# Attention products on two row halves of TensorE, padded leftovers and two pairs of heads at a time, in a linear-attention plus gated-FFN kernel

## The chip, the cores and the metric

One core of one Trainium2 chip runs the whole program. The metric is the device time of one execution in microseconds (us). Most executions agree within 0.3%. A profiled execution's span is about 1.8 us shorter than its measured time (838.4 against 840.17 for the kernel before).

## The reference

```python
kv  = einsum('bhsd,bhse->bhde', k, v)            # batch 8, heads 8, 576 tokens, 64 per head
out = einsum('bhsd,bhde->bhse', q, kv)
out = out / sqrt(mean(out*out, -1) + 1e-6) * g_norm
x   = out.transpose(0, 2, 1, 3).reshape(4608, 512)
h   = ((x @ w1) * (x @ w2)) @ w3                 # w1, w2: 512x1024, w3: 1024x1024
y   = h @ w_out                                  # 1024x512
```

All is fp32. 576 tokens are 512 plus a leftover of 64. The kernel folds `w3 @ w_out` into one 1024x512 matrix first (the "fold"), then runs eight tiles of 512 tokens and one of the eight leftovers through the FFN ("gates" and "projection", by a Winograd scheme of 2x2 blocks). The attention of the next batch is cut into pieces that stand between the gate matmuls. Batch 0's attention stands in the second half of the fold.

## The kernel before

Heads come in pairs (`r`, two heads `e`). k·v runs on two column halves of the array, one head each; the leftover has 64 rows:

```python
def kv(r):
    ...
    for j in range(J + 1):                     # 4 blocks of 128 tokens, then the leftover
        for e in range(2):
            nc.tensor.matmul(kv_ps[e * D:(e + 1) * D, :],
                lhsT=k_sb[:, e, cols] if j < J else kl_sb[:, 2 * r + e, :],   # kl_sb: 64 rows
                rhs=v_sb[:, e, cols] if j < J else vl_sb[:, 2 * r + e, :],
                start=(j == 0), stop=(j == J))
    ...                                        # copied twice, onto the diagonal of bd
```

q·kv uses that block-diagonal matrix, so that one full-array matmul serves two sets of 128 tokens, half of its products being with zeros:

```python
def product(r):
    o_ps = bank(ps_at, "at")
    for e in range(2):
        for i in range(2):
            n = 2 * e + i
            nc.tensor.matmul(o_ps[:, n * P:(n + 1) * P],
                lhsT=qT[r][:, e, i, :],        # 128 x 128
                rhs=bd[:, 2 * r + e, :],       # 128 x 128, block-diagonal
                start=True, stop=True)
    ...
    return norm(...)      # square, sum, root, reciprocal, scale: ScalarE and VectorE
```

The pieces of one batch, in the order in which they stand between gate matmuls (`begin`: k·v and the q transposes, `middle`: product and normalization, `turn`: transposes of the result), and batch 0's places among the eight steps of the fold:

```python
pieces = [[(begin, 0)], [(middle, 0), (begin, 1)], [(turn, 0), (middle, 1)], [(begin, 2), (turn, 1)],
          [(middle, 2), (begin, 3)], [(turn, 2), (middle, 3)], [(turn, 3)], []]
AT = {1: 0, 3: 1, 4: 2, 5: 3}      # fold step: pair of batch 0
ps_mm = ... bufs=5                 # PSUM banks for fold, gates and projection
ps_at = ... bufs=3                 # PSUM banks for attention and transposes
```

PSUM is the memory into which TensorE writes its results. The kernel takes it in eight tiles of 512 columns, here called banks.

## Time and profile before

| | before |
|---|---|
| median time | 839.25 us (3 runs; 839.14 with the rounds of the comparison) |
| span of the profile | 838.4 us |
| TensorE busy | 98% |
| VectorE, ScalarE busy | 46%, 32% |
| first gate matmul starts at | 91.16 us |
| from there to the end | 747.2 us |

The last two rows split the time at the first gate matmul. Ahead of it (the "start") weights are loaded and converted and the fold is done, with TensorE, VectorE and the DMA near their limits (from 16 to 49 us they are busy for 32.67, 31.02 and all of the 33 us). After it (the "main part") TensorE runs almost without a gap. Where a matmul stands in time is read from the timeline; the distance from one start to the next is its price, since matmuls are pipelined and a record's own length is a latency.

### The profile page before, as it was taken

What the parts mean: (1) busy time and instruction counts of PE and PEld (TensorE: products, weight loads), DVE (VectorE), ACT (ScalarE), POOL (GpSimd) and SP (SyncE); (2) the same over time, 40 slices, a digit from 0 to 9 for tenths busy, and PEclk for the clock granted to TensorE, in tenths of its full rate; (3) what the DMA queues carried; (4) which work ended last, traced back from release to release, by engine and by line L of the source; (5) the groups of instructions that cost most, each with busy time, mean ns of one, the idle gap of its engine ahead of it and who ended that gap; (6) DMA issues with size and microseconds to landing.
All of it is one profiled execution on the core that took longest, in us unless ns stands there. A gap on an engine that the chain in (4) does not pass through costs nothing.

```text
span 838.4 us, 11142 instructions
## 1 busy us (share of the span) xinstructions
PE 824.1 (98%) x4556; PEld 697.2 (83%) x4556; DVE 384.5 (46%) x770; ACT 268.5 (32%) x507; POOL 0.7 (0%) x6
## 2 busy tenths in 40 slices
PE   6999999999999999999999999999999999999997
PEld 4455788888888888888888888888888888888886
DVE  7978996415431544154315441453145404422430
ACT  5668443223312332133223321332133312211210
POOL 0000000000000000000000000000000000000000
PEclk9999999999999999999999999999999999999999
DMA  8999232022203220113022301230120010001002
GB/s 306 323 281 288 68 89 86 3 89 70 57 0 100 70 58 1 76 52 87 1 78 62 88 2 51 76 88 1 51 76 1 1 51 1 0 1 51 1 0 51
DMA packets 60002, 59.44 MB, mean 71 GB/s; under 512 B 15408, under 2 KB 56368, under 8 KB 59952
## 3 DMA queue, kind: packets, MB, share of 16 engines
q1 hardware_dynamic: 59792, 58.73, 22.6%
q8 instruction: 36, 0.59, 0.3%
q14 instruction: 14, 0.11, 0.1%
q10 hardware_dynamic: 160, 0.00, 0.0%
HBM read 49.28 MB, written 9.44 MB: 70 GB/s over the span
## 4 chain that ended last, share of the span: by engine, by line
PE 95%; DMA 2%; DVE 1%; ACT 1%; issue 0%; SPq 0%; ACTq 0%; DVEq 0%
PE mm L464 78%; PE mm L445 5%; PE at L337 3%; PE at L270 3%; PE at L292 2%; PE at L367 2%; DMA raw<-in_moe_w_out_dram 1%; DMA raw<-in_moe_w_dram 1%; PE at L354 1%; PE at L432 1%; DVE ab L151 0%; SPq L184 0%; PE at L376 0%; PE at L302 0%; DVE chunks L158 0%
## 5 line engine op out<-in xcount | busy, mean ns | idle before, releaser
L464 PE MATMUL mm<-xT,w_sb 128*128 128x256 f32 x768 | 176.2, 379 | 0.0
L464 PEld LDWEIGHTS mm<-xT,w_sb 128*128 128x128 f32 x768 | 145.9, 190 | 20.3 <-issue 0.5
L464 PE MATMUL mm<-xc,ws 128*128 128x256 f32 x576 | 130.2, 379 | 0.0
L464 PEld LDWEIGHTS mm<-xc,ws 128*128 128x128 f32 x576 | 109.4, 190 | 14.9
L477 ACT COPY u<-mm 128x512 f32<-128x512 f32 x90 | 52.8, 586 | 205.3 <-PE mm L464 190.6
L477 ACT COPY p<-mm 128x512 f32<-128x512 f32 x90 | 52.7, 586 | 138.9 <-PE mm L464 138.8
L464 PE MATMUL mm<-w3o_sb,ab 128*128 128x256 f32 x432 | 96.2, 379 | 0.0
L464 PEld LDWEIGHTS mm<-w3o_sb,ab 128*128 128x128 f32 x432 | 82.1, 190 | 11.2
L464 PE MATMUL mm<-xc,w_sb 128*128 128x256 f32 x288 | 68.1, 379 | 0.0
L445 PE MATMUL mm<-chunks,ab 128*128 128x512 f32 x128 | 62.6, 624 | 4.1 <-DVE chunks L161 4.1
L464 PE MATMUL mm<-raw 128*128 128x256 f32 x288 | 63.6, 379 | 0.0
L464 PEld LDWEIGHTS mm<-raw 128*128 128x128 f32 x288 | 54.7, 190 | 7.4
L464 PE MATMUL mm<-xT,ws 128*128 128x256 f32 x256 | 60.8, 380 | 0.0
L312 DVE TENSOR_REDUCE inv<-sq 128x8 f32<-128x512 f32 (+1 forms) x40 | 25.1, 629 | 73.3 <-ACT sq L310 73.3
L464 PEld LDWEIGHTS mm<-xc,w_sb 128*128 128x128 f32 x288 | 52.9, 190 | 6.2
L590 DVE TENSOR_TENSOR c<-mm,u 128x512 f32<-128x512 f32 x36 | 24.5, 681 | 61.2 <-PE mm L464 61.2
L464 PEld LDWEIGHTS mm<-xT,ws 128*128 128x128 f32 x256 | 46.5, 190 | 5.4
L619 DVE TENSOR_TENSOR raw<-mm,u 128x512 f32<-128x512 f32 x9 | 6.2, 692 | 97.3 <-PE mm L464 97.3
L591 DVE TENSOR_TENSOR ab<-c 128x256 f32<-128x256 f32 x108 | 45.6, 423 | 2.9
L445 PEld LDWEIGHTS mm<-chunks,ab 128*128 128x128 f32 x128 | 23.1, 200 | 27.3 <-issue 21.9
L590 DVE TENSOR_TENSOR c<-p,u 128x512 f32<-128x512 f32 x36 | 24.9, 691 | 34.3 <-ACT u L477 34.3
L284 DVE COPY kv_bd<-at 64x64 f32<-64x64 f32 x64 | 13.9, 217 | 55.8 <-PE at L270 55.2
(83 smaller groups left out, 856.6 us busy)
## 6 DMA issues: line engine op xcount, KB each, us to landing
raw<-in_moe_w_dram SPq DMA_DIRECT2D x31, 512.0 KB, 6.6
k_sb<-in_k_dram SPq DMA_DIRECT2D x32, 256.0 KB, 2.8
v_sb<-in_v_dram SPq DMA_DIRECT2D x32, 256.0 KB, 3.2
q_sb<-in_q_dram SPq DMA_DIRECT2D x32, 256.0 KB, 4.3
out_dram<-raw SPq DMA_DIRECT2D x16, 512.0 KB, 2.6
raw<-in_moe_w_out_dram SPq DMA_DIRECT2D x8, 512.0 KB, 8.3
kl_sb<-in_k_dram SPq DMA_DIRECT2D x8, 128.0 KB, 4.9
vl_sb<-in_v_dram SPq DMA_DIRECT2D x8, 128.0 KB, 4.6
```

What stands on the lines that cost most here:

```text
L270: nc.tensor.matmul(kv_ps[e * D:(e + 1) * D, :], lhsT=k_sb[:, e, cols] if j < J else kl_sb[:, 2 * r + e, :], rhs=v_sb[:, e, cols] if j < J ...
L284: nc.vector.tensor_copy(out=dst, in_=src)
L292: nc.tensor.transpose(qt_ps[:, e, i, :], q_sb[:, e, i * P:(i + 1) * P], ident)
L312: nc.vector.tensor_reduce(out=inv, in_=sq[:, cols].rearrange("p (h d) -> p h d", d=D), axis=AX.X, op=ALU.add,)
L337: nc.tensor.matmul(o_ps[:, n * P:(n + 1) * P], lhsT=qT[r][:, e, i, :], rhs=bd[:, 2 * r + e, :], start=True, stop=True,)
L354: nc.tensor.matmul(o_ps[l * L:(l + 1) * L, r * D:(r + 1) * D], lhsT=st["qT"][rows, r, l * L:(l + 1) * L], rhs=kv_bd[l][rows, 2 * r + e, rows],
L367: nc.tensor.transpose(t_ps[:, j, :], st[r][:, j], ident)
L445: nc.tensor.matmul(sums_ps[half][m], lhsT=w3T[half, c][:, m, :], rhs=chunks[:, c, 1, :], start=(c == 0), stop=(c == KF - 1),)
L464: nc.tensor.matmul(ps[:, u, :], lhsT=lhsT(a_name, u, c), rhs=rhs(b_name, c),  start=(u == 0 and c == 0 and to is None), stop=(c == chunks ...
L477: nc.scalar.copy(t, ps)
L590: nc.vector.tensor_add(c, one, two)
L591: nc.vector.tensor_mul(dst, c[:, 0, :], c[:, 1, :])
```

## The change

The author's intent: a contraction of 64 rows wastes half of a 128-row array, so run two of them at once on the two row halves, drop the zeros of the block-diagonal form, pad the leftover of k and v with zero rows so that its k·v needs no other array layout, and treat two pairs of heads at a time so that layouts change less often. The diff, cut to its core:

```diff
+    kv_left = [const.tile([P, H, D], FP32, name=f"{name}l_sb") for name in "kv"]
+    for t in kv_left:
+        nc.gpsimd.memset(t[L:P], 0.0)                 # rows 64 to 127 are zero
-    kv_bd = [const.tile([P, H, P], ...)]; memset
+    kv_sb = [const.tile([P, 2, NP, D], FP32, name=f"kv_sb{i}") for i in range(2)]
 def kv(rs):                                           # rs: two pairs (one in batch 0)
-                        rhs=v_sb[:, e, cols] if j < J else vl_sb[:, 2 * r + e, :],
+                            rhs=v_sb[:, e, cols] if j < J else vl[:, 2 * r + e, :],   # 128 rows
 def product(h):                                       # h: two pairs
-            o_ps = bank(ps_at, "at")
+            o_ps = [bank(ps_at, "at") for _ in range(2)]
+            for m in range(4):
+                r, e = 2 * h + m // 2, m % 2
+                for i in range(2):
+                    for l in range(2):                # row half
+                        rows = slice(l * D, (l + 1) * D)
+                        n = 2 * m + i
+                        nc.tensor.matmul(o_ps[l][:, n * D:(n + 1) * D],
+                            lhsT=qT[r][rows, e, i, :], rhs=kv_b[rows, e, r, :], ...)
 def product_left():                                   # leftover q, four 64x64 tiles
-            for e in range(2): ... for l in range(2): for r in range(NP):
+            for r in range(NP): for l in range(2): for e in range(2):
 def norm(o_ps, dsts):                                 # now over two banks, one root for both
-            [(begin, 0)], [(middle, 0), (begin, 1)], [(turn, 0), (middle, 1)], [(begin, 2), (turn, 1)],
-            [(middle, 2), (begin, 3)], [(turn, 2), (middle, 3)], [(turn, 3)], [],
+            [(begin, 0, 1)], [(middle, 0)], [(turn, 0), (turn, 1)], [(begin, 2, 3)],
+            [(middle, 1)], [(turn, 2), (turn, 3)], [], [],
-        AT = {1: 0, 3: 1, 4: 2, 5: 3}
+        AT = {1: 0, 2: 1, 4: 2, 5: 3}                 # product after every second pair
```

(Cuts throughout; indices and copies that follow from these are left out.)

More of the change, by code (lines that the diff above doesn't have):

```diff
@@ L84 @@
     q_left = {}
-    kv_left = {}
+    kv_left = [const.tile([P, H, D], FP32, name=f"{name}l_sb") for name in "kv"]
+    for t in kv_left:
+        nc.gpsimd.memset(t[L:P], 0.0)
     def load_pair(b, r):
@@ L99, in load_kv_left @@
     def load_kv_left(b):
-        kv_left[b] = []
-        for name, src in (("k", k), ("v", v)):
-            t = inp.tile([L, H, D], FP32, name=f"{name}l_sb", bufs=1)
-            nc.sync.dma_start(out=t, in_=src[b, :, G:S, :].rearrange("h p d -> p h d"))
-            kv_left[b].append(t)
+        for t, src in zip(kv_left, (k, v)):
+            nc.sync.dma_start(out=t[0:L], in_=src[b, :, G:S, :].rearrange("h p d -> p h d"))
     def load_q_left(b):
@@ L240 @@
     nc.vector.memset(eps_col, 1e-6)
-    kv_bd = [const.tile([P, H, P], FP32, name=f"kv_bd{i}") for i in range(2)]
-    for t in kv_bd:
-        nc.vector.memset(t, 0.0)
+    kv_sb = [const.tile([P, 2, NP, D], FP32, name=f"kv_sb{i}") for i in range(2)]
     g_col = const.tile([P, 1], FP32, name="g_col")
@@ L257, in attention, with kv @@
     def attention(b):
-        bd = kv_bd[b % 2]
+        kv_b = kv_sb[b % 2]
         qT = {}
         x = xT[b] = work.tile([P, 2, 2, NP // 2, N], FP32, name="xT")
-        def kv(r):
-            k_sb, v_sb, _ = loaded[b, r]
-            kl_sb, vl_sb = kv_left[b]
-            kv_ps = bank(ps_at, "at")[:, 0:D]
-            for j in range(J + 1):
-                cols = slice(j * D, (j + 1) * D)
-                for e in range(2):
-                    nc.tensor.matmul(
-                        kv_ps[e * D:(e + 1) * D, :],
-                        lhsT=k_sb[:, e, cols] if j < J else kl_sb[:, 2 * r + e, :],
-                        rhs=v_sb[:, e, cols] if j < J else vl_sb[:, 2 * r + e, :],
-                        start=(j == 0),
-                        stop=(j == J),
-                    )
-            for i in range(2):
-                rows = slice(i * D, (i + 1) * D)
-                for e in range(2):
-                    dst, src = bd[rows, 2 * r + e, rows], kv_ps[e * D:(e + 1) * D]
-                    if i:
+        def kv(rs):
+            n = len(rs)
+            kv_ps = bank(ps_at, "at")[:, 0:n * D].rearrange("p (r d) -> p r d", d=D)
+            for r in rs:
+                k_sb, v_sb, _ = loaded[b, r]
+                kl, vl = kv_left
+                for j in range(J + 1):
+                    cols = slice(j * D, (j + 1) * D)
+                    for e in range(2):
+                        nc.tensor.matmul(
+                            kv_ps[e * D:(e + 1) * D, r - rs[0], :],
+                            lhsT=k_sb[:, e, cols] if j < J else kl[:, 2 * r + e, :],
+                            rhs=v_sb[:, e, cols] if j < J else vl[:, 2 * r + e, :],
+                            start=(j == 0),
+                            stop=(j == J),
+                        )
+            for e in range(2):
+                for i in range(2):
+                    dst = kv_b[i * D:(i + 1) * D, e, rs[0]:rs[0] + n, :]
+                    src = kv_ps[e * D:(e + 1) * D]
+                    if e:
                         nc.scalar.copy(dst, src)
@@ L303, in q_t_left, with norm @@
             nc.scalar.copy(st["qT"], qt_ps)
-        def norm(o_ps, dst):
-            n, m = dst.shape[1:3]
-            cols = slice(0, n * m * D)
-            sq = work.tile([P, G], FP32, name="sq", bufs=1)
-            nc.scalar.activation(sq[:, cols], o_ps[:, cols], AF.Square)
-            inv = work.tile([P, H], FP32, name="inv")[:, 0:n * m]
-            nc.vector.tensor_reduce(
-                out=inv,
-                in_=sq[:, cols].rearrange("p (h d) -> p h d", d=D),
-                axis=AX.X,
-                op=ALU.add,
-            )
+        def norm(o_ps, dsts):
+            n, w = len(o_ps), o_ps[0].shape[1]
+            inv = work.tile([P, n, w // D], FP32, name="inv")
+            for i in range(n):
+                sq = work.tile([P, G], FP32, name="sq", bufs=1)[:, 0:w]
+                nc.scalar.activation(sq, o_ps[i], AF.Square)
+                nc.vector.tensor_reduce(
+                    out=inv[:, i], in_=sq.rearrange("p (h d) -> p h d", d=D), axis=AX.X, op=ALU.add
+                )
             yield
@@ L321, in norm @@
             nc.vector.reciprocal(inv, inv)
-            nc.vector.tensor_tensor(
-                out=dst,
-                in0=o_ps[:, cols].rearrange("p (n m d) -> p n m d", m=m, d=D),
-                in1=inv.rearrange("p (n m) -> p n m", m=m).unsqueeze(3).to_broadcast(
-                    [P, n, m, D]
-                ),
-                op=ALU.mult,
-            )
-        def product(r):
-            o_ps = bank(ps_at, "at")
-            for e in range(2):
-                for i in range(2):
-                    n = 2 * e + i
-                    nc.tensor.matmul(
-                        o_ps[:, n * P:(n + 1) * P],
-                        lhsT=qT[r][:, e, i, :],
-                        rhs=bd[:, 2 * r + e, :],
-                        start=True,
-                        stop=True,
-                    )
-            st[r] = work.tile([P, J, 2, D], FP32, name="xn", bufs=3)
-            return norm(o_ps, st[r].rearrange("p j e d -> p e j d"))
@@ L347, in product_left @@
-        def product_left():
-            xn = st["left"] = work.tile([P, H, D], FP32, name="xn", bufs=3)
-            for e in range(2):
-                o_ps = bank(ps_at, "at")
-                rows = slice(e * D, (e + 1) * D)
-                for l in range(2):
-                    for r in range(NP):
+            for i in range(n):
+                m, k = dsts[i].shape[1:3]
+                nc.vector.tensor_tensor(
+                    out=dsts[i],
+                    in0=o_ps[i].rearrange("p (m k d) -> p m k d", k=k, d=D),
+                    in1=inv[:, i].rearrange("p (m k) -> p m k", k=k).unsqueeze(3).to_broadcast(
+                        [P, m, k, D]
+                    ),
+                    op=ALU.mult,
+                )
@@ L354, in product_left, with product @@
+        def product(h):
+            o_ps = [bank(ps_at, "at") for _ in range(2)]
+            for m in range(4):
+                r, e = 2 * h + m // 2, m % 2
+                for i in range(2):
+                    for l in range(2):
+                        rows = slice(l * D, (l + 1) * D)
+                        n = 2 * m + i
                         nc.tensor.matmul(
-                            o_ps[l * L:(l + 1) * L, r * D:(r + 1) * D],
-                            lhsT=st["qT"][rows, r, l * L:(l + 1) * L],
@@ L357, in product_left @@
-                            rhs=kv_bd[l][rows, 2 * r + e, rows],
+                            o_ps[l][:, n * D:(n + 1) * D],
+                            lhsT=qT[r][rows, e, i, :],
+                            rhs=kv_b[rows, e, r, :],
                             start=True,
@@ L360, in product_left @@
                         )
-                all_of(norm(o_ps, xn.rearrange("p (r e) d -> p r e d", e=2)[:, :, e:e + 1, :]))
+            xn = st[h] = work.tile([P, 2, 2, 4, D], FP32, name="xn")
+            return norm(o_ps, [xn[:, :, l].rearrange("p i m d -> p m i d") for l in range(2)])
+        def product_left():
+            xn = st["left"] = work.tile([P, NP, 2, D], FP32, name="xn_left", bufs=1)
+            o_ps = [bank(ps_at, "at") for _ in range(2)]
+            for r in range(NP):
+                for l in range(2):
+                    for e in range(2):
+                        rows = slice(e * D, (e + 1) * D)
+                        nc.tensor.matmul(
+                            o_ps[e][l * L:(l + 1) * L, r * D:(r + 1) * D],
+                            lhsT=st["qT"][rows, r, l * L:(l + 1) * L],
+                            rhs=kv_sb[l][rows, e, r, :],
+                            start=True,
+                            stop=True,
+                        )
+            o_ps = [t[:, 0:NP * D] for t in o_ps]
+            all_of(norm(o_ps, [xn[:, :, e:e + 1, :] for e in range(2)]))
         def turn(r):
             t_ps = bank(ps_at, "at").rearrange("p (j t) -> p j t", j=J)
+            m = 2 * (r % 2)
             for j in range(J):
-                nc.tensor.transpose(t_ps[:, j, :], st[r][:, j], ident)
+                nc.tensor.transpose(t_ps[:, j, :], st[r // 2][:, j // 2, j % 2, m:m + 2, :], ident)
             dst = x[:, r // 2, :, r % 2, :]
@@ L376, in turn_left @@
                 nc.tensor.transpose(
-                    t_ps[:, r // 2, r % 2, :], st["left"][:, 2 * r:2 * r + 2, :], ident
+                    t_ps[:, r // 2, r % 2, :], st["left"][:, r], ident
                 )
@@ L381, in turn_left, with middle, begin @@
             nc.scalar.activation(dst, t_ps, AF.Copy, scale=g_col)
-        def middle(r):
-            all_of(product(r))
-        def begin(r):
-            kv(r)
-            q_t(r)
-            if r + 2 < NP:
-                load_pair(b, r + 2)
-            elif b + 1 < B:
-                load_pair(b + 1, r + 2 - NP)
-                if r + 1 == NP:
-                    load_kv_left(b + 1)
-                    if b == 0:
-                        load_q_left(1)
+        def middle(h):
+            all_of(product(h))
+        def begin(*rs):
+            kv(rs)
+            for r in rs:
+                q_t(r)
+                if r + 2 < NP:
+                    load_pair(b, r + 2)
+                elif b + 1 < B:
+                    load_pair(b + 1, r + 2 - NP)
+                    if r + 1 == NP:
+                        load_kv_left(b + 1)
+                        if b == 0:
+                            load_q_left(1)
         if b == 0:
@@ L400, in attention @@
         pieces = [
-            [(begin, 0)],
-            [(middle, 0), (begin, 1)],
-            [(turn, 0), (middle, 1)],
-            [(begin, 2), (turn, 1)],
-            [(middle, 2), (begin, 3)],
-            [(turn, 2), (middle, 3)],
-            [(turn, 3)],
+            [(begin, 0, 1)],
+            [(middle, 0)],
+            [(turn, 0), (turn, 1)],
+            [(begin, 2, 3)],
+            [(middle, 1)],
+            [(turn, 2), (turn, 3)],
+            [],
             [],
@@ L675 @@
                 begin(AT[c])
-            if c - 1 in AT:
+            if c - 1 in norms:
                 all_of(norms[c - 1])
@@ L690 @@
             if c in AT:
-                norms[c] = product(AT[c])
-                next(norms[c])
-                next(norms[c])
-            if c - 1 in AT:
+                if AT[c] % 2:
+                    norms[c] = product(AT[c] // 2)
+                    next(norms[c])
+                    next(norms[c])
+            if c - 1 in norms:
+                turn(AT[c - 1] - 1)
                 turn(AT[c - 1])
```

## The prediction

> **What bounds the kernel now.** I read the page's first two parts, then the groups of instructions by form, then the waits of the matmul engine and the chain of waits, and last the timeline around one attention piece.
>
> ```profile
> PE 824.1 (98%) x4556; PEld 697.2 (83%) x4556; DVE 384.5 (46%) x770; ACT 268.5 (32%) x507; POOL 0.7 (0%) x6
> ...
> PE 95%; DMA 2%; DVE 1%; ACT 1%; issue 0%; SPq 0%; ACTq 0%; DVEq 0%
> ...
> L337 PE MATMUL at<-kv_bd,qT 128*128 128x128 f32 x256 | 33.8, 275 | 0.0
> L270 PE MATMUL at<-v_sb,k_sb 128*64 128x64 f32 x512 | 21.9, 228 | 0.7 <-ACT ab L437 0.7
> L270 PE MATMUL at<-vl_sb,kl_sb 64*64 64x64 f32 x128 | 10.6, 242 | 0.0
> L354 PE MATMUL at<-kv_bd,qT_left 64*64 64x64 f32 x128 | 6.1, 224 | 0.0
> ```
>
> TensorE is busy 98% of 838.4 us and makes 95% of the chain that ended last. VectorE and ScalarE have more than half of the span free. So a change pays by the TensorE time that it removes, and costs by any new TensorE wait. Attention is a small part: the four groups shown hold 72.4 us together. The transposes around them stay as they are.
>
> The mean of one matmul is a latency; the price is the distance between starts. The timeline gives it:
>
> ```profile
> 189.23 1.05 PE L337 MATMUL at<-kv_bd,qT 128*128 128x128 f32 x8
> 190.22 0.69 PE L270 MATMUL at<-v_sb,k_sb 128*64 128x64 f32 x16
> 190.83 0.33 PE L270 MATMUL at<-vl_sb,kl_sb 64*64 64x64 f32 x4
> 191.09 0.66 PE L292 MATMUL at<-ident,q_sb 128*128 128x128 f32 x4
> 191.59 1.89 PE L464 MATMUL mm<-xc,w_sb 128*128 128x256 f32 x8
> ...
> 198.50 0.60 PE L367 MATMUL at<-ident,xn 128*128 128x128 f32 x4
> 198.94 1.06 PE L337 MATMUL at<-kv_bd,qT 128*128 128x128 f32 x8
> 199.83 1.89 PE L464 MATMUL mm<-xT,ws 128*128 128x256 f32 x8
> ```
>
> A source fp32 matmul leaves two records, each with its own weight load; a transpose leaves one. Four q·kv products (8 records) take 199.83 − 198.94 = 0.89 us when a full-array matmul follows, and 0.99 when a 64-column one does: entering another layout of the array costs 0.10. The 16 records of k·v take 0.61 us, 38 ns each; the four leftover ones take 0.26, 65 ns each. The four transposes take 0.50 after the narrow layout, 0.44 otherwise (198.94 − 198.50).
>
> Single records of the trace split these further. Inside the k·v group two records, one per column half, start 6 ns apart, and such couples follow every 58 ns. The first couple of a layout waits 50 ns more for its weights, and leaving the layout takes 90. So 0.61 is 0.05 + 8 × 0.058 + 0.09, and 0.26 is 0.05 + 2 × 0.058 + 0.09: in the leftover group most is switching.
>
> **What the Trainium skill says.** "TensorEngine Tiling (Array Packing)", section Tiling Modes, Key Properties: a change of the tiling mode drains TensorE, and tiles may load weights and multiply in parallel. The trace agrees on both (0.10 us in, 0.09 out; couples 58 ns apart). "TensorE: Matmul & The Clock Gate", section LDWEIGHTS: load time goes with the columns of the weights, not with the contraction rows. The trace agrees: loads of 64 columns show means of 137 ns with 128 rows and 131 with 64 rows, loads of 128 columns 190 ns, and the first full-width load after a switch delays its matmul by 104 ns. The same page, Part 3, describes tiles in different row groups as running at once; no instruction of this trace uses two row halves at full column width, so that is not shown here. The same page, Part 1: an idle window halves the clock for a few microseconds. The trace has one case, below.
>
> **The change part by part.**
>
> *k·v by two pairs, leftover padded to 128 rows.* Per two pairs the old path is 2 × (0.10 + 0.61 + 0.26 + 0.50) = 2.94 us. The new one is one switch in (0.10), one exposed load (0.05), 20 couples × 0.058 = 1.16, one way out (0.09), one exposed transpose load (0.06), eight transposes at 0.109 = 0.87: 2.33. It saves 0.61 us, and there are 14 such pieces in batches 1 to 7: −8.5. Batch 0 keeps one pair at a time and loses only the leftover's layout, 0.15 × 4: −0.6.
>
> *q·kv on two row halves.* Old, per two pairs: 2 × 0.89 = 1.78, with no switch. New: a pair has 8 source matmuls, 16 records, so 8 couples of one record for each row half; two pairs make 16 couples. The moving side halves to 64 columns (about 53 ns by the k·v pitch), but each half still loads 128 weight columns per record, which took about 107 ns: 104 exposed above, and the old product's pitch of 0.89/8 = 111 ns, against 109 for a transpose of the same width, is already that of its loads. So I take 111 ns per couple: 16 × 0.111 = 1.78, the same as before. The halving of the matmul time is hidden behind the weight loads. On top comes a round trip of layout that did not exist: 0.10 in, 0.104 first load, 0.09 out, 0.104 for the first load of the next full matmul: 0.40. Sixteen pieces (14 and two in batch 0): +6.4.
>
> *Leftover q product.* Old: 32 records in 163.05 − 161.58 = 1.47 us, tile after tile at 58 ns. New order goes round the four 64x64 tiles, so they run side by side: between 8 × 0.058 = 0.46 and 32 × 0.029 = 0.93 (29 ns is what k·v is seen to issue at); with switches kept, about 0.65 saved, four times: −2.6.
>
> *VectorE and ScalarE.* Fewer copies (64 copies of 217 ns on VectorE become half as many, twice as wide), fewer square roots; worth nothing by itself. But one normalization now serves two pairs, with one squares buffer, so it becomes square, sum, square, sum, root, reciprocal, two scalings. From the old durations, starting 0.26 after the product: 0.60 + 0.70 + 0.60 + 0.70 + 0.35, reciprocal 0.2, two scalings 0.6 each, and about 1.0 of gate work that the order of instructions puts between: some 5.5 us. The transposes after the second half of a batch come 5.18 us after the product (24 gate records of 0.216). That leaves a wait of 0.2 to 0.5, seven times, and a somewhat longer one in the crowded first tile: +2.5 in all.
>
> *The start, 49 to 92 us.* TensorE waits here twice:
>
> ```profile
> 72.60 0.60 PE L367 MATMUL at<-ident,xn 128*128 128x128 f32 x4
> 73.91 0.69 PE L270 MATMUL at<-v_sb,k_sb 128*64 128x64 f32 x16 [0.71 <-ACT ab L437]
> 74.52 0.33 PE L270 MATMUL at<-vl_sb,kl_sb 64*64 64x64 f32 x4
> 76.03 1.06 PE L292 MATMUL at<-ident,q_sb 128*128 128x128 f32 x4 [1.18 <-ACT xT L369]
> 76.89 4.06 PE L445 MATMUL mm<-chunks,ab 128*128 128x512 f32 x6
> ```
>
> The chain of waits over the same time, and the busy times of 76.1 to 79.5 us (after the five engines: granted clock, DMA share, GB/s):
>
> ```profile
> 64.44 7.70 DMA raw<-in_moe_w_dram
> ...
> 72.22 0.60 ACT w_sb L149
> ...
> 73.29 0.57 ACT ab L437
> ```
> ```profile
> 76.10:79.50 3.40, 3.40 (x8) 1.84 (x9) 3.30 (x6) 2.69 (x5) 0.00 (x0) 0.51 0.80 229
> ```
>
> A weight load that took 7.70 us held ScalarE, which held TensorE for 1.9 us, after which the clock was 0.51 for 3.4 us, another 1.7 lost. The change issues the last pair of batch 0 one step earlier, before that weight load, and the conversion ahead of it no longer waits behind a product. I expect this stall of 3.6 to vanish mostly: −2.5. Against it the two longer normalizations end about 4.9 us after their product where the next transposes stand at 3.96: +0.8 each, +1.6.
>
> **Sum.** −8.5 − 0.6 + 6.4 − 2.6 + 2.5 − 2.5 + 1.6 = −3.7 us. From 839.25 that is 835.5 us.
>
> **The rivals.** *The loads don't bind.* If the two halves follow each other at the 58 ns of k·v, a product costs 16 × 0.058 + 0.40 = 1.33 in place of 2.18: another −13.6, 822 us. For it speaks the intent of the change, against it the 104 ns load after a switch and the 190 against 137 ns of the load records. *The halves take turns.* If weights reach only one row half at a time, a couple costs 0.22: 16 × 16 × 0.11 = +28, 864 us. Against it: in the leftover product one tile begins while the tile of the other row half still runs, 6 ns apart at one place, with neither slowed; but those tiles differ in columns too. *The longer normalization becomes the bound.* If gate work pushes it 1.5 us past the transposes in each of 14 pieces, and the clock falls after some, +15 to +25, about 855. VectorE's 46% speaks against it, the exact order on a first-in-first-out queue for it. *The start decides.* The saved stall may turn into another (two norms, weight loads later), −4 to +5.
>
> **Range and chances.** 2% is 16.8 us. The main sum stays within it unless the couple pitch is at one of the extremes. I give the fast pitch 10%, taking turns or large waits together 7%. The range of 826 to 845 leaves a tenth on each side.
>
> **What would show it.** Right: the new q·kv group's 16-couple block takes about 2.0 us to the next gate matmul, its weight loads keep about 190 ns at 128 columns; the 40-record k·v block takes about 1.3; no 64-row k·v form is left; transposes of the second half show idle of some tenths before them, released by VectorE's scalings; the waits at 73.9 and 76.0 are gone or small. Wrong: a block of about 1.3 us (loads hidden) or 3.5 (taking turns), TensorE waits of over 10 us in sum, or a clock under 0.99 after 92 us.

## The result, and the profile after

The changed kernel takes 837.81 us (median of 4 runs, 836.86 to 839.72) against 839.14 in the same rounds. The ratio is 0.9989, 95% interval 0.9968 to 1.0011. Ratios here are the mean time of one kernel's fast runs over that of the other's of the same rounds, so not quite the ratio of the medians. The interval includes 1, so the total alone doesn't show a gain. The time is inside the predicted range, but 3.7 us were forecast and 1.3 came.

The engines of the changed kernel, and its attention rows by form:

```profile
PE 819.3 (98%) x4812; PEld 689.8 (82%) x4812; DVE 376.6 (45%) x720; ACT 259.6 (31%) x459; POOL 1.7 (0%) x8
```
```profile
L342 PE MATMUL at<-kv_sb,qT 64*128 64x64 f32 x512 | 32.0, 275 | 0.0
L272 PE MATMUL at<-v_sb,k_sb 128*64 128x64 f32 x512 | 20.5, 225 | 0.0
...
L272 PE MATMUL at<-vl_sb,kl_sb 128*64 128x64 f32 x128 | 9.2, 222 | 0.0
```

The figure with the star gives the rows and columns of the stationary side. q·kv is now 64 rows by 128 columns, twice as many records, and hardly less busy time (32.0 us where it was 33.8). The 64-row k·v form is gone.

The main part, around one batch's first half, in the changed kernel's timeline (start, length, engine, line):

```profile
353.83 0.69 PE L272 MATMUL at<-v_sb,k_sb 128*64 128x64 f32 x16
354.35 0.29 PE L272 MATMUL at<-vl_sb,kl_sb 128*64 128x64 f32 x4
354.46 0.64 PE L272 MATMUL at<-v_sb,k_sb 128*64 128x64 f32 x16
354.93 0.29 PE L272 MATMUL at<-vl_sb,kl_sb 128*64 128x64 f32 x4
355.15 1.09 PE L294 MATMUL at<-ident,q_sb 128*128 128x128 f32 x8
356.08 1.89 PE L473 MATMUL mm<-xT,ws 128*128 128x256 f32 x8
357.81 3.62 PE L473 MATMUL mm<-xT,w_sb 128*128 128x256 f32 x16
361.35 2.00 PE L342 MATMUL at<-kv_sb,qT 64*128 64x64 f32 x32
363.28 1.99 PE L473 MATMUL mm<-xc,w_sb 128*128 128x256 f32 x8
365.12 1.89 PE L473 MATMUL mm<-xT,w_sb 128*128 128x256 f32 x8
```

Two pairs' k·v and transposes take 356.08 − 353.83 = 2.25 us plus 0.10 on entering: 2.35, predicted 2.33. The product takes 363.28 − 361.35 = 1.93, plus 0.09 on entering (16 gate matmuls from 357.81 on would end at 361.26) and 0.11 in the next gate group (1.84 to its follower, where eight usually take 1.73): 2.13, predicted 2.18. No wait stands anywhere in these lines. The leftover q product takes 316.94 − 316.31 = 0.63 us where it took 1.47:

```profile
316.31 0.69 PE L360 MATMUL at<-kv_sb,qT_left 64*64 64x64 f32 x32
316.94 1.99 PE L473 MATMUL mm<-xT,ws 128*128 128x256 f32 x8
```

So the main part went as planned and better: 836.8 − 94.61 = 742.2 us, 5.0 less than before. The start took it back. First the kernel before, then the changed one, at the end of the fold:

```profile
87.29 0.60 PE L367 MATMUL at<-ident,xn 128*128 128x128 f32 x4
87.73 3.60 PE L445 MATMUL mm<-chunks,ab 128*128 128x512 f32 x8
91.16 1.89 PE L464 MATMUL mm<-xT,w_sb 128*128 128x256 f32 x8
```
```profile
88.50 2.26 PE L375 MATMUL at<-ident,xn 128*128 128x128 f32 x8 [2.39 <-DVE xn L323]
90.56 4.21 PE L454 MATMUL mm<-chunks,ab 128*128 128x512 f32 x8
94.61 1.89 PE L473 MATMUL mm<-xT,w_sb 128*128 128x256 f32 x8
```

TensorE waited 2.39 us for VectorE's scaling of a product, and then ran at half clock. From start to start the eight transposes take 2.06 us (0.87 in the main part) and the eight fold records 4.05 (3.43 in the kernel before), so the half clock lost another 1.8. The chain of waits of the changed kernel tells what made that scaling late:

```profile
67.41 0.68 DVE xn L323
68.09 1.13 DVE ab L151
...
73.94 6.91 DMA raw<-in_moe_w_dram
80.88 1.16 ACT w_sb L149
...
83.39 1.22 DVE ab L151
84.61 0.59 DVE inv L314
85.21 1.13 DVE w_sb L161
86.34 0.61 DVE inv L314
...
87.67 1.30 DVE xn L323 x2
```

Read from the top: the normalization of the first two pairs (its scaling, L323) stands ahead of a weight conversion (L151) in VectorE's order. The conversions free the buffers of the next weight loads late. Counted in order of issue, the same pair of loads leaves SyncE's queue (SPq) at 70.50 in the kernel before and at 73.52 in the changed one:

```profile
70.50 0.92 SPq L184 DMA_DIRECT2D raw<-in_moe_w_dram  x2
```
```profile
73.52 0.93 SPq L184 DMA_DIRECT2D raw<-in_moe_w_dram  x2
```

The later load of the pair starts at 73.94 and lands at 80.9, and its conversion stands between the two sums (L314) of the next two pairs' normalization, for which TensorE waits.

A second part of the 3.45 us is older: the first attention matmul of batch 0 starts at 50.93 in place of 49.69. The busy times of two stretches of the changed kernel, then of one of the kernel before (after the five engines: granted TensorE clock, DMA share, GB/s):

```profile
16.70:20.10 3.40, 3.40 (x5) 1.30 (x4) 3.33 (x5) 2.63 (x3) 0.00 (x0) 0.50 1.05 377
88.40:91.80 3.40, 3.24 (x10) 2.40 (x11) 3.33 (x6) 1.69 (x3) 0.00 (x0) 0.50 0.51 170
```
```profile
11.30:14.70 3.40, 3.18 (x4) 1.52 (x5) 2.28 (x4) 2.83 (x3) 0.00 (x0) 0.50 1.05 377
```

Both kernels have one half-clock stretch of 3.4 us in the early fold. Before, it fell on the first six fold matmuls, after which TensorE had to wait for the next weights anyway (0.42 us there, 2.00 us in the changed kernel, whose first six ran at full clock). In this execution of the changed kernel it fell on dense fold matmuls.

### The profile page after: what moved, and what is told of

Same layout as the page of the kernel before. It is cut to its first block, busy times and chain, and to the rows that moved or that the text cites. A ratio compares the mean times of both kernels' runs of the same rounds, so it can differ in the third digit from the quotient of the medians.

```text
span 836.8 us, 11539 instructions
## 1 busy us (share of the span) xinstructions
PE 819.3 (98%) x4812; PEld 689.8 (82%) x4812; DVE 376.6 (45%) x720; ACT 259.6 (31%) x459; POOL 1.7 (0%) x8
## 4 chain that ended last, share of the span: by engine, by line
PE 94%; DVE 2%; DMA 2%; ACT 1%; issue 0%; SPq 0%; DVEq 0%; ACTq 0%
PE mm L473 78%; PE mm L454 5%; PE at L342 3%; PE at L272 2%; PE at L375 2%; PE at L294 2%; DMA raw<-in_moe_w_out_dram 1%; DMA raw<-in_moe_w_dram 1%; PE at L441 1%; DVE ab L151 1%; PE at L304 0%; DVE inv L314 0%; PE at L360 0%; ACT qT L296 0%; SPq L184 0%
## 5 line engine op out<-in xcount | busy, mean ns | idle before, releaser
L314 DVE TENSOR_REDUCE inv<-sq 128x8 f32<-128x512 f32 (+1 forms) x40 | 25.3, 632 | 68.2 <-ACT sq L313 68.2
L313 ACT ACTIVATE sq<-at 128x512 f32<-128x512 f32 (+1 forms) x40 | 22.2, 555 | 47.9 <-PE at L342 32.6
```

Source lines behind the costliest of these rows:

```text
L313: nc.scalar.activation(sq, o_ps[i], AF.Square)
L314: nc.vector.tensor_reduce(out=inv[:, i], in_=sq.rearrange("p (h d) -> p h d", d=D), axis=AX.X, op=ALU.add)
```

## The experiments

I had two questions. In the main part: is it really the weight loads that keep the row halves from paying (theory A), or something else (rival B)? And the start: is the loss the first batch's new scheme, or chance in the clock? Since the main part repeats to 0.02 us between profiles of equal code (742.20, 742.20 and 742.22 us in three kernels that differ in the start alone), the split at the first gate matmul is the sharpest reading. A median start is worked out as median time − 1.8 − main part.

| kernel | median us (runs) | ratio to before, 95% interval | first gate matmul, profile | main part | median start |
|---|---|---|---|---|---|
| before | 839.14 | | 91.16 | 747.2 | 90.1 |
| changed | 837.81 (4) | 0.9989, 0.9968 to 1.0011 | 94.61 | 742.2 | 93.8 |
| blockdiag | 830.81 (4) | 0.9903, 0.9885 to 0.9920 | 93.02 | 737.4 | 91.6 |
| moving128 | 839.19 (4) | 0.9998, 0.9980 to 1.0016 | 94.76 | 743.0 | 94.4 |
| first_single | 842.71 (6) | 1.0041, 1.0021 to 1.0060 | 97.90 | 742.2 | 98.7 |
| best | 829.24 (5) | 0.9888, 0.9871 to 0.9905 | 90.33 | 737.4 | 90.0 |
| unpadded | 843.50 (4) | 1.0048, 1.0035 to 1.0061 | 93.31 | 748.4 | 93.3 |
| left_old | 839.89 (4) | 1.0017, 1.0002 to 1.0032 | 91.06 | 745.6 | 92.5 |
| ident_first | 838.52 (6) | 0.9986, 0.9972 to 1.0000 | 93.62 | 742.2 | 94.5 |
| at_shift | 837.31 (6) | 0.9979, 0.9966 to 0.9991 | 93.36 | 742.2 | 93.3 |
| hybrid | 834.40 (6) | 0.9950, 0.9935 to 0.9965 | 89.36 | 742.2 | 90.4 |
| banks44 | 836.26 (6) | 0.9962, 0.9946 to 0.9977 | 91.32 | 740.4 | 94.1 |
| best_banks44 | 825.36 (5) | 0.9841, 0.9828 to 0.9854 | 88.88 | 735.7 | 87.9 |

**blockdiag: only the product put back to 128 rows.**

```diff
-  o_ps[l][:, n*D:(n+1)*D], lhsT=qT[r][rows, e, i, :], rhs=kv_b[rows, e, r, :]    # l: row half
+  o_ps[p][:, n*P:(n+1)*P], lhsT=qT[r][:, e, i, :],    rhs=bd[:, r, e, :]         # p: pair
```

(With it go what the form needs: copies of kv onto a zeroed block diagonal, and another order of the products in the banks and in `xn`.)

> The changed kernel with only the q kv product put back to 128-row contractions against block-diagonal kv (still by two pairs of heads). Theory A (weight loads of 128 columns set the pitch at about 111 ns, so the row halves gain nothing and cost a round trip of array layout): the product falls from about 2.13 us to 1.78 us per two pairs, 16 times, so 5.6 us less than the changed kernel, about 832 us; the start up to the first gate matmul stays late (near 94 us). Rival B (the row halves do save matmul time): slower than the changed kernel by 5 us or more.

It takes 830.81 us, so 7.0 less than the changed kernel, of which 4.8 in the main part (14 pieces: 0.34 each, 0.35 expected) and the rest in the start. Its timeline at one product:

```profile
297.83 1.95 PE L342 MATMUL at<-kv_bd,qT 128*128 128x128 f32 x16
299.62 1.89 PE L478 MATMUL mm<-xT,ws 128*128 128x256 f32 x8
```

16 records in 1.79 us where the row halves need 32 in 1.93 plus both switches. Rival B is out: the row halves cost time here.

**moving128: twice the moving columns, wrong result.**

```diff
-  o_ps[l][:, n * D:(n + 1) * D],               rhs=kv_b[rows, e, r, :]
+  o_ps[l][:, min(n, 6)*D:(min(n, 6) + 2)*D],   rhs=kv_b[rows, e, 2*h:2*h + 2, :]
```

> Wrong result on purpose: the changed kernel with the moving side of each row-half product doubled from 64 to 128 columns, everything else the same. Theory A (weight loads bind): the 32-record block keeps its 1.93 us and the time stays within 1.5 us of the changed kernel, about 838 us. Rival B (the matmul streaming sets the pitch): 16 couples grow by up to 53 to 107 ns each in 16 pieces, 14 to 27 us more, 852 to 865 us.

```profile
301.70 2.06 PE L342 MATMUL at<-kv_sb,qT 64*128 64x128 f32 x32
303.69 1.99 PE L473 MATMUL mm<-xT,ws 128*128 128x256 f32 x8
```

The same 32 records with 128 moving columns take 1.99 us in place of 1.93. Doubling the work that the change had halved costs 0.06 us a block, 0.8 us in the main part. So the streaming doesn't set the pace, and theory A stands. In single records of the changed kernel's trace the couples follow every 112 ns (fourteen steps in 1.56 us). The rows didn't matter either: with 128 weight columns the pitch is 111 ns in the full array and 109 for transposes, with 64 columns it is 58 ns at 128 rows (k·v) and at 64 rows (leftover q). No run changed the columns of the weights alone.

**unpadded: the leftover of k and v with 64 rows again.**

```diff
-  lhsT=... else kl[:, 2 * r + e, :]
+  lhsT=... else kl[0:L, 2 * r + e, :]       # and vl alike
```

> The changed kernel with only the padding undone (the leftover k and v contract over 64 rows again). By the terms of the prediction each piece of two pairs then leaves and enters another layout four more times in place of none: about 0.42 us more in 14 pieces and 0.15 in the four of batch 0, 6.5 us in sum, about 844 us. If switching is hidden beside other work: no change.

```profile
355.16 0.69 PE L272 MATMUL at<-v_sb,k_sb 128*64 128x64 f32 x16
355.77 0.33 PE L272 MATMUL at<-vl_sb,kl_sb 64*64 64x64 f32 x4
356.04 0.69 PE L272 MATMUL at<-v_sb,k_sb 128*64 128x64 f32 x16
356.65 0.33 PE L272 MATMUL at<-vl_sb,kl_sb 64*64 64x64 f32 x4
356.91 1.09 PE L294 MATMUL at<-ident,q_sb 128*128 128x128 f32 x8
357.84 1.89 PE L473 MATMUL mm<-xT,ws 128*128 128x256 f32 x8
```

The block takes 2.68 us in place of 2.25, and the main part 6.2 more (14 × 0.43 is 6.0). Multiplying the zero rows costs nothing that shows: the four padded records take 0.11 us (354.35 to 354.46), 58 ns a couple as the others. Leaving the layout is what cost. Of the 8.3 us that the k·v part saves in the main part, the padding is thus the larger share.

**left_old: the leftover q product tile after tile again** (loops `e, l, r` in place of `r, l, e`).

> The changed kernel with only the loop order of the leftover q product put back (tile after tile in place of round the four tiles). The trace shows 0.63 us for the block in place of 1.47, four times: 3.4 us more than the changed kernel, about 841 us, and the block back at 1.4 to 1.5 us.

The block is back at 1.47 us (0.63 in the changed kernel), and the main part is 745.6, 3.4 more, exactly as expected. The total came out 1.3 lower than expected, since in its runs the start was early: its profile has no half-clock stretch after the fold's beginning, and gates at 91.06. The start's code is that of the changed kernel, whose gates came at 94.61, so one profile of a start is good to some ±2 us only.

**ident_first: the identity matrix built before the padding memsets.** On GpSimd the two memsets delayed the warm-up matmuls from 1.4 to 2.4 us.

> The changed kernel with the identity matrix built ahead of the two padding memsets, so that the warm-up matmuls begin at 1.4 to 1.9 us in place of 2.4. Theory (the half-clock window at 16.7 us of the changed kernel's profile falls where it falls, and the first weight load hides the memsets): no change, 837.8 within 1 us. Rival: the memsets moved that window, and the time falls by 1.2 to 1.6 us.

838.52 us: no gain. Where the first half-clock stretch begins differs between kernels whose code up to there is the same (10.6, 12.1, 13.5 and 16.7 us in first_single, unpadded, moving128 and the changed kernel). So the 1.2 us that the changed kernel's profile lost before 51 us can be put down to chance; its runs spread by 2.9 us. The later half clock isn't certain either: in ident_first a wait of 2.58 us for the same scalings was followed by a clock of 1.00.

**first_single: batch 0 by single pairs at the old steps, still on row halves.**

```diff
-  AT = {1: 0, 2: 1, 4: 2, 5: 3}        # product(h) after every second pair
+  AT = {1: 0, 3: 1, 4: 2, 5: 3}        # product(h, (pair,)) after every pair, row halves kept
```

> The changed kernel with only the first batch put back to one pair of heads per product and normalization, at the old steps; its row halves stay. Theory A (the start lost 3.5 us because a normalization of two pairs delays the weight conversion behind it and is delayed by it): first gate matmul at 92 to 93 us in place of 94.6, the wait of 2.4 us before the transposes gone, total 836 us, although two more layout round trips cost 0.8. Rival C (the start differs by where the clock windows fall, not by the pairing): first gate matmul stays at 94 or later, total 838.

A miss: 842.71 us, gates at 97.90. Its timeline in the fold:

```profile
66.23 0.69 PE L272 MATMUL at<-v_sb,k_sb 128*64 128x64 f32 x16 [0.36 <-ACT ab L447]
...
68.76 1.12 PE L294 MATMUL at<-ident,q_sb 128*128 128x128 f32 x4 [1.73 <-DMA raw<-in_moe_w_dram]
...
78.75 1.05 PE L272 MATMUL at<-v_sb,k_sb 128*64 128x64 f32 x16 [2.23 <-ACT xT L378]
...
81.07 1.12 PE L294 MATMUL at<-ident,q_sb 128*128 128x128 f32 x4 [1.06 <-ACT kv_sb L284]
```

A product on row halves writes two banks, even for one pair, and attention has three. With a product after every pair the next pair's k·v and transposes find no bank until ScalarE and VectorE have finished with the last. The waits end as such a bank comes free: at 68.76 and 81.07 when ScalarE's copies of kv are done (68.71 and 81.01; the first line names a DMA, but the last semaphore before its transposes is ScalarE's), at 78.75 after its copy of xT (78.70). No run gave this kernel more banks, so this is read from one trace. So pairing by itself isn't the fault: with two banks per product, the pairing is even the better way. That part of my theory fell.

**at_shift: batch 0 in steps 1, 2, 3, 4** in place of 1, 2, 4, 5.

> The changed kernel with the second half of the first batch one step earlier in the fold (steps 1, 2, 3, 4 in place of 1, 2, 4, 5). Theory (the transposes wait at 86 to 88.5 us because the normalization of two pairs stands behind a conversion whose weight load landed at 80.9): with the normalization a step earlier that wait of 2.4 us shrinks or moves, gates start at about 92 to 93 us, total 835 to 836. Rival (the conversions set the pace whatever the place of the attention): gates start at 94 to 95, total 838.

837.31 us, no different from the changed kernel. The wait of 2.4 us at 88.5 was gone, but one of 2.9 us before the q transposes had taken its place (released by ScalarE's copies of kv). Moving the attention moves the wait.

**best: block-diagonal products, batch 0 by single pairs, all else of the change kept.** (blockdiag, plus the old `AT` with a one-bank product after every pair, plus ident_first.)

> Block-diagonal 128-row products throughout, kv by two pairs with padded leftovers, new leftover order, first batch as before one pair at a time, identity matrix built ahead of the padding memsets. If the parts add up: 839.1 minus 8.5 (kv) minus 3.4 (leftover product) minus 0.6 (padding in batch 0), about 826.6 us, first gate matmul at 90.5 to 91.5 us. If the start is a matter of clock windows, 828 to 830.

829.24 us. The main part is blockdiag's 737.4; the median start is 90.0 in place of 91.6. It was placed at 826.6 by adding up the terms, which left out the waits for banks shown below.

**hybrid: only batch 0 put back**, one bank, one pair, block-diagonal (its k·v leftovers stay padded), while batches 1 to 7 stay as changed.

> The changed kernel with only its first batch put back whole: one pair of heads at a time at the old steps, block-diagonal 128-row product in one bank, while batches 1 to 7 keep row halves and pairs of pairs. Theory (the missing 3.5 us are the first batch's scheme): everything after the first gate matmul keeps 742.2 us, that matmul comes at 89.5 to 91.5 us as in the kernel before, about 834.0 us. Rival (they are clock windows and chance): 837 to 838.

834.40 us, with a main part of 742.2 and gates at 89.36:

```profile
85.46 0.63 PE L402 MATMUL at<-ident,xn 128*128 128x128 f32 x4 [0.34 <-DVE xn L327]
85.92 3.60 PE L481 MATMUL mm<-chunks,ab 128*128 128x512 f32 x8
89.36 1.89 PE L500 MATMUL mm<-xT,w_sb 128*128 128x256 f32 x8
```

The wait of 2.39 us is down to 0.34. Its runs end at 832.8 to 837.5, the changed kernel's at 836.9 to 839.7: nearly apart. The intervals of the two ratios to the kernel before don't meet (0.9935 to 0.9965, 0.9968 to 1.0011). So the loss belongs in the main to the first batch's new scheme, with the half clock that its wait can bring, and not to chance alone: about 3.4 us by the medians. How much each of its parts (pairing, two banks, two more layout switches, the step) gives is not settled: blockdiag, which keeps the pairs, starts at 91.6 by its median, halfway.

**banks44 and best_banks44: four PSUM banks for attention, four for the gates** (`ps_mm` 4, `ps_at` 4 in place of 5 and 3). Two pairs' `begin` takes all three attention banks, so the leftover q transposes behind it wait: the changed kernel's waits of TensorE show it, and a stretch of its timeline; then the same stretch in banks44.

```profile
PE at L304 <- ACT qT L296: 1.0, 4, 0.2
```
```profile
113.28 1.09 PE L294 MATMUL at<-ident,q_sb 128*128 128x128 f32 x8
114.61 0.66 PE L304 MATMUL at<-ident,ql_sb 128*128 128x128 f32 x4 [0.24 <-ACT qT L296]
115.11 1.89 PE L473 MATMUL mm<-xT,ws 128*128 128x256 f32 x8
```
```profile
110.00 1.09 PE L294 MATMUL at<-ident,q_sb 128*128 128x128 f32 x8
110.92 0.60 PE L304 MATMUL at<-ident,ql_sb 128*128 128x128 f32 x4
111.36 1.89 PE L473 MATMUL mm<-xT,ws 128*128 128x256 f32 x8
```

> The changed kernel with PSUM shared out as four banks for the gates and four for attention in place of five and three. Theory (two banks per product leave too few): the four waits of 0.24 us before the leftover q transposes go, so the part after the first gate matmul falls from 742.2 to about 741.2; in the start it helps little, since that wait is for VectorE's scalings. 836 to 837. Rival: four gate banks are too few and the gates wait, 840 or more.

> The fastest version so far (829.24) with the same four and four banks. The waits of 0.24 us go (1.0 us), and the wait of 1.3 us for a bank at 75 us in its start with the half clock that follows it may go too: 826 to 828. Rival: the gates wait for banks, 832 or more.

From the first q transpose to the next gate matmul it is 1.83 us with three banks and 1.36 with four: a wait noted as 0.24 us costs 0.47. In single records 0.16 of the rest lie under the pipelined end of the record before, and about 0.06 are the first transpose's exposed weight load. Four of these are 1.9, and the main part fell by 1.8, not by the 1.0 that I had read off the waits. The gates didn't miss their fifth bank. best_banks44 takes 825.36 us, ratio 0.9841, and beats both kernels; its start is early too, since the wait for a bank at 75 us and the half clock after it are gone.

## Why the prediction was right or wrong

Its size was wrong, by the term for the start; the mechanism of the main part was right. That the total lies within the range is partly luck: the main part came out 2.0 us better than predicted and the start some 4 worse. Term by term, for the main part as measured by taking each part back:

| term | predicted | measured | by |
|---|---|---|---|
| k·v by two pairs, padded, 14 pieces | −8.5 | −8.3 | 14 × (2.94 − 2.35) |
| q·kv on row halves, 14 pieces (of 16) | +5.6 | +4.8 | blockdiag |
| leftover q product | −2.6 | −3.4 | left_old |
| longer normalization | +2.5 | 0 | no such wait |
| bank waits in batches with leftover q | not seen | +1.8 | banks44 |
| main part | −3.0 | −5.0 | profiles |
| start | −0.7 | about +3.4 to +3.7 | hybrid; medians |

- *Weight loads bind the row halves.* Right: a couple of records takes about the 111 ns that I took from the old full-array product. moving128 and blockdiag show it from both sides.
- *A round trip of layout costs 0.40 us.* About right: 2.13 measured for the block against 2.18.
- *Leftover product.* Its direction was right and its size low: four tiles run fully side by side (0.46 us of streaming), where I had allowed for the issue rate to bind.
- *Longer normalization, +2.5.* Wrong, narrowly. After the product that ends at 303.15 in the changed kernel the scalings of both banks end at 308.2, and the transposes stand at 308.44. I had put 5.5 us against 5.18; it was some 5.1 against 5.3, the second because the next gate group is longer by its exposed weight load.
- *Bank waits.* I had not counted that two pairs' `begin` fills the three attention banks just ahead of the leftover q transposes.
- *The start: this is the step that failed.* "I expect this stall of 3.6 to vanish mostly: −2.5" stood against two longer normalizations that "end about 4.9 us after their product where the next transposes stand at 3.96: +0.8 each, +1.6". The old stall of 0.71 and 1.18 us did vanish, though the reason given misread the diff: the last pair of batch 0 stays at step 5, and it is the second that moves, from 3 to 2. The first normalization was as predicted: its scalings end at 68.09, 4.85 us after the product, and cost two waits of 0.26 and 0.20. The second was not: its scalings end at 88.96, 6.99 us after the product. The first had pushed VectorE's conversions back, these the weight loads, and a conversion then stood inside the second: one wait of 2.39 us with a half-clock stretch, the same kind of stall 12 us later. In place of −0.7 the start came to +3.7 by the medians. I had written this down as a rival ("The start decides", −4 to +5) and left it at the favourable end in the sum. Putting batch 0 back (hybrid) returns 3.4 us.
- *Smaller slips.* The 190 against 137 ns of the load records was no evidence for the columns: loads of 128 columns for transposes show 141. A clock of half speed has not one case in the trace of the kernel before but also the stretch at 11.3 us. And a sign of being wrong came true by its words, "TensorE waits of over 10 us in sum": the changed kernel's list adds up to 11.5 us (8.3 before), but all except the 1.0 before the leftover q transposes lie ahead of the first gate matmul.

So of the 5.0 us that the main part gained, 3.7 were given back in the start by the medians, and 1.3 remained.

## What to carry to other kernels

Before you split a contraction over row halves, compare the columns of the weight load with the columns that stream: with each load used once and 128 columns wide, halving the stream gained nothing here, and the new layout cost its switches. Padding with zero rows to stay in one layout cost nothing that showed and was worth 6 us. In a section where several engines and the DMA are near their limits, don't credit a stall as gone until you know what the engines' order puts in its place, and count the PSUM banks of every piece that will stand side by side.

## What the Trainium skill lacked or had wrong

- "TensorEngine Tiling (Array Packing)", Theoretical Speedup and When to Use Tiling: up to 2x for a contraction of 64 or less. It doesn't say that the gain is lost where weights of 128 columns are loaded for each short matmul: here 2.13 us per two pairs against 1.78 in the full array.
- The same page, Key Properties: it says that a change of mode drains TensorE, without a price. Here about 0.10 us to enter and 0.09 to leave, plus the first weight load exposed, some 0.05 us at 64 columns and 0.10 at 128.
- "TensorE: Matmul & The Clock Gate", Part 3, has matmuls start in strict program order. The block of the leftover q product in the kernel before, eight records on each of four tiles in turn, takes 1.47 us; at the 58 ns of a record on its own tile, a strict order would need at least 28 × 0.058 = 1.62, even if each tile began together with the last record of the one before. In single records the second tile begins at 161.87 while the first tile's go on every 58 ns up to 162.04.
- The same page, Part 1: the clock halves after an idle window of about 3.4 us. Here waits of 2.39 us (changed kernel) and of 0.71 and 1.18 close together (before) were followed by a clock of 0.50 for 3.4 us; waits of 2.58 (ident_first) and 2.00 (banks44) at the same place were not.
- No page that I read says that an idle gap shown before a record understates the loss: 0.24 us shown, 0.47 lost.
